# A Fourier mixing and low-rank mixer kernel: first joins of batch 0 in two pieces, one PSUM bank of the front under another tag, and a few steps of batches 1 and 2 at other places in the order

## The chip, the cores and the metric

The program runs on one core of one Trainium2 chip. The metric is the device time of one execution in microseconds (us), lower is better; several executions are summed up by their median. The engines are called as in the profile: PE (TensorE, matmuls), PEld (its weight loads), DVE (VectorE), ACT (ScalarE), POOL (GpSimd) and SP (SyncE, which here only issues DMAs).

## What is computed

`x` has the shape (8, 3136, 256) in float32, with `U` (3136, 32), `V` (32, 3136), `w_ch1` (256, 1024) and `w_ch2` (1024, 256).

```python
X = np.fft.fft(x, axis=1)
X = np.fft.fft(X, axis=2)
x = X.real.astype(np.float32)

xt = x.transpose(0, 2, 1)
h = xt @ U @ V
u = x + h.transpose(0, 2, 1)
ch = np.maximum(u @ w_ch1, 0.0) @ w_ch2
out = (u + ch).astype(np.float32)
```

## The kernel before

**Tiling.** The transform is written as matmuls with sine and cosine tables. For each of the 8 batches DVE first folds the rows of `x` (tiles `xf`, `xr`) by symmetry into `eof`, `eor`, `eos`, `ge`, `go` and `gc`; PE multiplies the folded rows by the tables into PSUM tiles named `pt`; ACT and DVE put these into two tiles `A` and `B` (bf16, 128 x 1569) and a small one, `tab`, for the low-rank product. In the odd half, `apart` makes `eh` on DVE from a copy `ev` of the first product, and `join` writes `pt + eh` and `pt - eh` into the upper parts of `A` and `B`. In the even half, `mirrored` does the same in one DVE instruction from `ev` and the second product. `chan` then transforms along the other axis (PE into `pst`, a copy to `S` or `T`), `lowrank` and `hidden` make the tiles `ta` and `qt` of the low-rank part, and `spread_rank` transposes `qt` into `qf` by a DMA transpose.

**Chunks.** The half-rows of all batches form chunks of 512 columns, counted by `c`. For each chunk `front` makes `u` = `ph` + `S` (or `T`) on DVE, one instruction for each of two halves, and starts a DMA transpose of `u` into `ut` on SP; `odd_part` makes `uo` = `S` - `T` on DVE; `direct` multiplies `u` by the first weights (PE into `p1`, ACT to `h`, line 866); `mirrors` adds `uo` and the low-rank part to the same banks (ACT to `h`, line 882); `second_product` multiplies `h` by the second weights, and DVE adds `ut` (lines 944 and 945) into `o`, which SP stores after a correction by POOL (`fx`, line 949).

**PSUM.** There are eight banks: tag `dft` has 2, `p1` has 4, `p2` has 2. A bank is given again when the last reader of its tile is done, so a matmul into a tag waits for that reader.

**Order.** Up to `order.close()` the program stands as it is written (a manual schedule): this is the front, batch 0 and the start of chunk 0. Behind it, a list of due slots (`due`, six for each chunk) says where a step of the transform of the next batch stands among the steps of the chunks: `turn(c, sl)` runs what `put` has placed at `6 * c + sl`. `transform(b)` gives the place of the first step and the list of steps; `FOLDS` gives the places of the folds. From there on PE keeps the order written; on the other engines a scheduler may move an instruction unless `tc.keep_in_program_order` pins it. `in_turn` makes `u` and `uo`, and pins them for the first chunks. `fold_tt` pins the folds.

**What the change touches.** `lrow` (line 146) lies in the pool `gen`, which `setup.close()` gives back before `cp`, the pool of `u`, `h`, `ut` and `o`, is opened; `places` (line 278) builds `EM` from `lrow` on POOL. `even_again` (line 669) makes again the first even product of batch 0, whose bank `mirrored(0, 1, cos_even)` reads. `first_u` (line 725) makes `u` of chunk 0 from columns 0 to 255 and 785 to 1040 of `A` and `B`. The DMA transposes wait for each other by semaphores, whichever queue issues them: the one of `qf` of batch 1 is issued by ACT, all the others by SP.

Of the kernel before, what the change touches and what calls it, by code (L numbers as in the profile page):

```python
# [20 lines left out]
NT = 196  # L21
# [5 lines left out]
QW = TE + NE  # L27
# [4 lines left out]
def kernel(  # L32
# [9 lines left out]
    nc = tc.nc  # L42
# [4 lines left out]
    HALF = S // 2  # L47
# [57 lines left out]
    BUFS = {"dft": 2, "p1": 4, "p2": 2}  # L105
# [37 lines left out]
    iota(jv[:], [[1, KP]], 0, 1)  # L143
    for q in (0, 2):
        load_f(x, xf, 0, q, D)
    lrow = gen.tile([P, 2, P], FP32, name="lrow")
    pcol = cpool.tile([P, 1], FP32, name="pcol")
    pint = cpool.tile([P, 1], I32, name="pint")
    iota(lrow[:], [[0, 2], [1, P]], 0)
# [128 lines left out]
    def places():  # L278

        nc.gpsimd.tensor_scalar(hm[:, 0:1], pcol[:], float(D), 0.0, op0=AL.mult, op1=AL.add)  # L280
        nc.gpsimd.tensor_scalar(hm[:, 1:2], pcol[:], -float(D), float(P), op0=AL.mult, op1=AL.add)
        for s in range(2):
            nc.gpsimd.tensor_scalar(EM[:, s * P:(s + 1) * P], lrow[:, 0, :], hm[:, s:s + 1], 1.0,
                                    op0=AL.is_equal, op1=AL.mult)
        nc.gpsimd.memset(EM[0:1, P:P + 1], 1.0)
# [164 lines left out]
    pinned = []  # L450
# [5 lines left out]

    def in_turn(c, *a, **k):
        ins = nc.vector.tensor_tensor(*a, **k)  # L458
        if pinned and c <= 2:
            tc.keep_in_program_order(ins)  # L460

    def mm(*a, **k):
# [82 lines left out]
    def seq(b, par, typ, pn, tag="dft", part=True):  # L545

        d = state(b)
        ne = NE if b else 0
        pt = psum.tile([P, QW + NE], FP32, tag=tag, name="pt", bufs=BUFS[tag])
        d["pt"] = pt  # L550
        todo = products(b, par, typ, P * typ, pn == 1, ne)
        if typ == 0 and b == 0:
            todo = todo + products(b, par, 1, 256, (pn == 1) == (par == 1), ne)
        elif typ == 0 and pn == 1:
            todo = todo + [(QW, w, rhs) for w, rhs in u_odd(b, 1, 256)]
        add_up(pt, todo)
        if pn == 0:
            ev = d["ev"] = wp.tile([P, QW], FP32, tag="ev", name="ev", bufs=EB)
            w = (2 * NT if par else TE) + ne
            nc.scalar.copy(ev[:, :w], pt[:, :w])  # L560
            if part:
                apart(b, par)

    def apart(b, par, kept=None):

        d = kept or ST[b]
        ne = NE if b else 0
        if par == 1:
            w, ev = 2 * NT + ne, d["ev"]
            eh = d["eh"] = wp.tile([P, 2 * NT], FP32, tag="eh", name="eh", bufs=2)  # L570
            nc.vector.tensor_tensor(eh[:, 0:NT], ev[:, NT - 1::-1], ev[:, w - 1:w - NT - 1:-1],
                                    op=AL.subtract)
            nc.vector.tensor_tensor(eh[:, NT:2 * NT], ev[:, 0:NT], ev[:, w - NT:w], op=AL.add)

    def join(b, par, typ, kept=None, low=True, high=True):

        d = kept or ST[b]
        ne = NE if b else 0
        pt, ev = d["pt"], d["ev"]
        dst = ST[b]["A"] if typ == 1 else ST[b]["B"]  # L580
        p_, e_ = pt[:, 0:2 * NT], d["eh"][:]
        up, dn = dst[:, 1176:784:-1], dst[:, 1177:HALF + 1]
        if low:
            nc.vector.tensor_tensor(up, p_, e_, op=AL.add)
        if not high:
            return
        if typ == 1:
            nc.vector.tensor_tensor(dn, e_, p_, op=AL.subtract)
        else:
            nc.vector.tensor_tensor(dn, p_, e_, op=AL.subtract)  # L590
        if ne:
            pu, eu = 2 * NT, NT
            nc.vector.tensor_tensor(ST[b]["tab"][:, typ, par, :].rearrange("p (g r) -> p g r", r=R),
                                    four(pt[:], pu), four(ev[:], eu), op=AL.add)
            if typ == 0:
                alt = dst[0:1, 786:HALF + 1:2]
# [33 lines left out]
    def mirrored(b, typ, kept):  # L630

        ne = NE if b else 0
        pt, ev = kept["pe"], kept["ve"]
        dst = ST[b]["A"] if typ == 1 else ST[b]["B"]
        nc.vector.scalar_tensor_tensor(strip(dst[:], 394, [[-1, 2], [2, NT]]),
                                       strip(ev[:], 1, [[NT + ne, 2], [1, NT]]), 2.0 if typ else -2.0,
                                       strip(pt[:], 1, [[NT + ne, 2], [1, NT]]),
                                       op0=AL.mult, op1=AL.subtract if typ else AL.add)
# [31 lines left out]
    def even_again(b, typ, kept):  # L670

        ev = wp.tile([P, QW], FP32, tag="ev", name="ev", bufs=EB)
        nc.scalar.copy(ev[:, :TE], kept["pe"][:, :TE])
        kept["pe"] = ev
        pt = kept["ve"] = psum.tile([P, QW], FP32, tag="p1", name="pt", bufs=BUFS["p1"])
        add_up(pt, products(b, 0, typ, P * typ, False, 0))

    def chan(b, ch, h, tag="dft", eng=None):
# [93 lines left out]

    def spread_rank(b):

        (nc.scalar if b == 1 else nc.sync).dma_start_transpose(out=QF[b % 2][:], in_=QT[:])

    def width(c):
        return min(CH, NCOL - c * CH)
# [172 lines left out]
    def transform(b):  # L951

        def odd_rows(typ, pn):
            seq(b, 1, typ, pn)
            if pn:
                join(b, 1, typ)

        def even(typ, pn):
            even_rows(b, typ, pn)
            if pn:  # L960
                mirrored(b, typ, ST[b])

        a = [lambda pn=pn: even(1, pn) for pn in range(2)]
        s = [lambda pn=pn: even(0, pn) for pn in range(2)]
        c = [lambda pn=pn: odd_rows(1, pn) for pn in range(2)]
        d = [lambda pn=pn: odd_rows(0, pn) for pn in range(2)]
        rank = [lambda: lowrank(b)]
        ch = [lambda ch=ch, h=h: chan(b, ch, h) for ch in range(2) for h in range(2)]
        q = [lambda: hidden(b)]
        if b == 1:  # L970
            return 11, [a[:1], c[:1] + a[1:], c[1:] + d[:1], s[:1] + d[1:] + s[1:],
                        [lambda ch=ch: chan(b, ch, 0, eng=nc.vector.tensor_copy) for ch in (1, 0)], ch[3:] + rank,
                        ch[1:2] + q + [lambda: spread_rank(b)]]
        if b == 2:
            return 23, [a[:1], a[1:] + c[:1], [], c[1:] + s[:1], s[1:], d[:1], d[1:], ch[:1], ch[1:2] + rank,
                        q, ch[2:3], ch[3:]]
        return 6 * (b * HALF // CH) - 15, [[x] for x in a + c + d[:1] + s + d[1:] + ch[:1] + rank + ch[1:2] + q + ch[2:]]

# [135 lines left out]
    msr = MSX[0:1].rearrange("p (l two) -> p l two", two=2)  # L1114
    nc.gpsimd.memset(msr[:, :, 0:1], -1.0)
    nc.gpsimd.memset(msr[:, :, 1:2], 1.0)
    places()
    mirror(1, slice(128, 256), AL.add)
    half(0, 1, slice(128, 256))
    seq(0, 1, 1, 0, "dft", False)  # L1120
# [3 lines left out]
    for c in range(2):  # L1124
        fourth(0, c, slice(128, 256))
    apart(0, 1, cos_odd)
    nc.gpsimd.memset(DV[:, 0:1], 0.0)
# [14 lines left out]
    load_r(x, xr, 1, 0, 2, D)  # L1142
    load_0f(1)
    mirrored(0, 0, sin_even)
    join(0, 1, 1, cos_odd, low=False)
    mirrored(0, 1, cos_even)
    nc.vector.tensor_tensor(WD[:], W1[:, 1, :], W1[:, 0, :], op=AL.subtract)
    nc.gpsimd.memset(WD[0:1], 0.0)

    due = {}  # L1150

    def put(slot, *steps):
        due.setdefault(slot, []).extend(steps)
# [113 lines left out]
```

## Time and profile before

| | |
|---|---|
| median of 3 runs | 437.91 us (436.92, 437.91, 439.9) |
| the profiled execution's own time | 436.31 us |
| its span, first to last instruction | 434.5 us |
| granted TensorE clock | 1.00 over the span |
| busy: PE, PEld | 423.8 us (98%), 284.4 us (65%) |
| busy: DVE, ACT, POOL | 319.8 us (74%), 292.2 us (67%), 125.5 us (29%) |
| DMA, mean over the span | 156 GB/s |
| chain that ended last, by engine | PE 80%, DVE 7%, DMA 7%, POOL 2% |

Times in rows are in us from the start of the span. A row of the timeline gives the start, the length, the engine, the line, the operation, out<-in, the shape and the count of equal instructions run together, and in brackets how long the engine was idle before it and what ended that. Names are cut at digits: `p` stands for `p1` and `p2`, `w` for both weights, `te`, `to` and `ts` are the tables. Matmuls overlap, and their ends are modelled, so the pace of PE is best read from one start to the next. A small q behind an engine (ACTq, SPq) marks work of its sequencer, as the issue of a DMA.

### The profile page before, as it was taken

Reading aid. Unit: us, or ns where it says so; the run is one execution under the profiler, and the core shown is the slowest. Engines: PE = TensorE matmul, PEld = TensorE weight load, DVE = VectorE, ACT = ScalarE, POOL = GpSimd, SP = SyncE. Lnnn points to the kernel's source line nnn. Section 1 sums busy time; section 2 is a strip of 40 time slices with the busy share of each in tenths; the row PEclk is TensorE's granted clock in tenths of the full one; section 3 lists DMA queues with packets and bytes.
Section 4 is the critical chain, followed back from the end, with each engine's and each line's share of the span. In section 5 each row is a group of like instructions: output and inputs, shape, how many; then the busy total and the mean of one; then the engine's idle time right before and its main releaser. Section 6 shows DMA issues by size and latency. Waiting matters only on the chain.

```text
span 434.5 us, 9406 instructions
## 1 busy us (share of the span) xinstructions
PE 423.8 (98%) x3508; PEld 284.4 (65%) x3508; DVE 319.8 (74%) x665; ACT 292.2 (67%) x633; POOL 125.5 (29%) x340
## 2 busy tenths in 40 slices
PE   5999999999999999999999999999999999999996
PEld 2774676666766766666766766666766766666675
DVE  8998989797898787769777787769777554353442
ACT  7958765666667657776667657776667657765751
POOL 8861323153234233323233142322223100011111
PEclk9999999999999999999999999999999999999999
DMA  7899798869779586727885376866334324334543
GB/s 208 210 198 217 163 273 111 203 151 244 147 163 271 102 211 177 199 74 191 175 223 155 86 181 104 217 159 146 74 88 136 100 74 113 88 122 121 122 126 121
DMA packets 89165, 67.83 MB, mean 156 GB/s; under 512 B 55402, under 2 KB 82430, under 8 KB 89118
## 3 DMA queue, kind: packets, MB, share of 16 engines
q1 hardware_dynamic: 83350, 52.79, 50.2%
q0 software_dynamic: 5472, 14.36, 13.5%
q8 instruction: 27, 0.44, 0.4%
q14 instruction: 20, 0.16, 0.1%
q10 hardware_dynamic: 296, 0.07, 0.1%
HBM read 28.86 MB, written 25.69 MB: 126 GB/s over the span
## 4 chain that ended last, share of the span: by engine, by line
PE 80%; DVE 7%; DMA 7%; POOL 2%; issue 1%; ACT 1%; SPq 0%; ACTq 0%; DVEq 0%; POOLq 0%
PE p L463 65%; PE pt L463 7%; PE pst L463 4%; DMA out_dram<-o 3%; DMA xf<-in_x_dram,xidx 2%; DVE eof L453 2%; PE ph L463 2%; DVE eor L453 2%; DMA ut<-u 1%; PE ptt L463 1%; POOL xf L57 1%; DVE u L458 1%; DVE eos L453 1%; ACT h L882 1%; PE pq L463 1%
## 5 line engine op out<-in xcount | busy, mean ns | idle before, releaser
L463 PE MATMUL p<-w,h 128*128 128x256 bf16 x1576 | 195.1, 273 | 0.0
L463 PEld LDWEIGHTS <-h 128*128 128x128 bf16 x1576 | 148.6, 98 | 39.7 <-issue 15.8
L882 ACT ACTIVATE h<-p 128x512 bf16<-128x512 f32 (+1 forms) x200 | 101.5, 595 | 83.9 <-PE p L463 77.7
L866 ACT ACTIVATE h<-p 128x512 bf16<-128x512 f32 (+1 forms) x200 | 101.8, 600 | 8.0 <-PE p L463 7.5
L463 PE MATMUL p<-u,w 128*128 128x512 bf16 (+1 forms) x400 | 93.2, 374 | 0.6 <-ACT h L882 0.4
L944 DVE TENSOR_TENSOR o<-p,ut 128x256 f32<-128x256 f32 (+1 forms) x95 | 39.6, 416 | 67.9 <-PE p L463 47.2
L949 POOL TENSOR_TENSOR o<-o,fx 128x2 f32<-128x2 f32 (+1 forms) x95 | 39.5, 416 | 155.5 <-DVE o L945 81.1
L463 PEld LDWEIGHTS <-w 128*128 128x128 bf16 x512 | 41.7, 97 | 37.8 <-issue 1.8
L463 PE MATMUL p<-uo,wd 128*128 128x512 bf16 (+1 forms) x200 | 50.8, 375 | 0.2
L458 DVE TENSOR_TENSOR u<-ph,T 128x512 bf16<-128x512 f32 (+23 forms) x63 | 34.3, 556 | 9.9 <-PE ph L463 7.9
L945 DVE TENSOR_TENSOR o<-p,ut 128x256 f32<-128x256 f32 (+1 forms) x95 | 38.9, 409 | 0.0
L453 DVE TENSOR_TENSOR eof<-xf 99x1016 bf16<-99x1016 f32 (+1 forms) x33 | 38.3, 1171 | 0.2 <-issue 0.2
L453 DVE TENSOR_TENSOR eor<-xr 99x1016 bf16<-99x1016 f32 (+1 forms) x34 | 38.4, 1143 | 0.0
L57 POOL DMA_INDIRECT xf<-in_x_dram,xidx x32 | 34.5, 1077 | 11.8 <-issue 6.7
L458 DVE TENSOR_TENSOR u<-ph,S 128x512 bf16<-128x512 f32 (+23 forms) x63 | 34.2, 554 | 0.8 <-PE ph L463 0.3
L840 POOL TENSOR_TENSOR fx<-ut 128x4 f32<-128x4 bf16 x48 | 16.0, 334 | 58.8 <-DMA ut<-u 58.8
L463 PEld LDWEIGHTS <-wd 128*128 128x128 bf16 x200 | 19.4, 98 | 13.0 <-issue 0.3
L463 PE MATMUL pt<-te,gc 98*128 98x229 bf16 (+1 forms) x196 | 24.4, 260 | 0.3 <-DVE u L458 0.3
L690 ACT CAST T<-pst 128x392 bf16<-128x392 f32 (+1 forms) x28 | 17.3, 619 | 7.3 <-PE pst L463 6.8
L463 PEld LDWEIGHTS <-gc 98*128 98x128 bf16 x220 | 19.3, 97 | 4.4 <-issue 0.7
L463 PEld LDWEIGHTS <-go 98*128 98x128 bf16 x216 | 16.5, 97 | 6.7 <-issue 0.4
L690 ACT CAST S<-pst 128x392 bf16<-128x392 f32 (+1 forms) x28 | 17.4, 623 | 3.9 <-PE pst L463 3.9
(187 smaller groups left out, 450.3 us busy)
## 6 DMA issues: line engine op xcount, KB each, us to landing
out_dram<-o SPq DMA_DIRECT2D x33, 512.0 KB
xr<-in_x_dram SPq DMA_DIRECT2D x15, 784.0 KB
out_dram<-o SPq DMA_DIRECT2D x8, 384.0 KB
out_dram<-o SPq DMA_DIRECT2D x8, 256.0 KB
out_dram<-o SPq DMA_DIRECT2D x10, 128.0 KB
xr<-in_x_dram SPq DMA_DIRECT2D x2, 392.0 KB
ut<-u SPq DMA_TRANSPOSE x48
vv<-vv SPq DMA_DIRECT2D x3, 196.0 KB
```

The source lines that it names most:

```text
L57: nc.gpsimd.indirect_dma_start(out_, None, bass.AP(t.tensor, t.offset, [[w, rows], [1, w]]), bass.IndirectOffsetOnAxis(idx, 0), element_of ...
L453: ins = nc.vector.tensor_tensor(*a, **k)
L458: ins = nc.vector.tensor_tensor(*a, **k)
L463: ins = nc.tensor.matmul(*a, **k)
L690: eng(to, pt[:, :n])
L840: nc.gpsimd.tensor_tensor(fx[:, :, 1], ut[:, 0:n, 0] if hf else ut[:, n:2 * n, 0], ut[:, n + 1:2 * n + 1, 0], op=AL.subtract)
L866: nc.scalar.activation(k["h", 0][q][:, j - 4 * q, :w], p1[:, :w], AF.Relu)
L882: nc.scalar.activation(k["h", 1][q][:, g, :w], k["p1"][g][:, :w][:, ::-1], AF.Relu)
L944: nc.vector.tensor_tensor(o[:, ts, 0:P], p2[:, :w, 0:P], ut[:rows, ts, 0:P], op=AL.add)
L945: nc.vector.tensor_tensor(o[:, ts, P:D], p2[:, :w, P:D], strip(ut[:rows], (CH // P + t0 + 1) * P, [[P, w], [-1, P]]), op=AL.add)
L949: nc.gpsimd.tensor_tensor(o[:, ts, cols], o[:, ts, cols], fx[:rows, ts, 1 - hf:], op=AL.add)
```

## The change

It has these parts:

1. `lrow` moves from the pool `gen` to `cpool`, and `places()` and the memset of `DV[:, 0:1]` on POOL move from the middle of the front to behind the last join of batch 0.
2. The lower joins of batch 0 (`up`, 392 columns) are cut at column 136: `[136:392]`, which `first_u` reads, comes first for `A` and for `B`; `[0:136]` of `B` follows at once, that of `A` after `first_u`.
3. `even_again` takes its bank from `p2` instead of `p1`.
4. Batch 1: the `eh` of the odd cosine product is made behind `mirrored` and pinned there; the DMA transpose of `qf` moves from slot 16.5 to 16.75 and is pinned on ACT.
5. Batch 2: the steps of the transform that stood at slots 23 and 24 move to 24 and 25, and the fold of `go`'s first half from 22 to 22.75 (the order of the folds stays).
6. `in_turn` pins `u` and `uo` for chunks 3 and 4 as well.

```diff
-    lrow = gen.tile([P, 2, P], FP32, name="lrow")
+    lrow = cpool.tile([P, 2, P], FP32, name="lrow")
...
     def in_turn(c, *a, **k):
         ins = nc.vector.tensor_tensor(*a, **k)
-        if pinned and c <= 2:
+        if pinned and c <= 4:
             tc.keep_in_program_order(ins)
...
-    def apart(b, par, kept=None):
+    def apart(b, par, kept=None, pin=False):
...
+            if pin:
+                tc.keep_in_program_order(ins)
...
-    def join(b, par, typ, kept=None, low=True, high=True):
+    def join(b, par, typ, kept=None, low=True, high=True, at=0, end=2 * NT):
...
-        up, dn = dst[:, 1176:784:-1], dst[:, 1177:HALF + 1]
+        up, dn = strip(dst[:], 1176, [[-1, 2 * NT]]), dst[:, 1177:HALF + 1]
         if low:
-            nc.vector.tensor_tensor(up, p_, e_, op=AL.add)
+            nc.vector.tensor_tensor(up[:, at:end], p_[:, at:end], e_[:, at:end], op=AL.add)
...
-        pt = kept["ve"] = psum.tile([P, QW], FP32, tag="p1", name="pt", bufs=BUFS["p1"])
+        pt = kept["ve"] = psum.tile([P, QW], FP32, tag="p2", name="pt", bufs=BUFS["p2"])
...
-        (nc.scalar if b == 1 else nc.sync).dma_start_transpose(out=QF[b % 2][:], in_=QT[:])
+        ins = (nc.scalar if b == 1 else nc.sync).dma_start_transpose(out=QF[b % 2][:], in_=QT[:])
+        if b == 1:
+            tc.keep_in_program_order(ins)
...
+        c0 = [lambda: seq(b, 1, 1, 0, part=False)]
...
         if b == 1:
-            return 11, [a[:1], c[:1] + a[1:], c[1:] + d[:1], s[:1] + d[1:] + s[1:],
+            return 11, [a[:1], c0 + a[1:] + [lambda: apart(b, 1, pin=True)], c[1:] + d[:1], s[:1] + d[1:] + s[1:],
                         [lambda ch=ch: chan(b, ch, 0, eng=nc.vector.tensor_copy) for ch in (1, 0)], ch[3:] + rank,
-                        ch[1:2] + q + [lambda: spread_rank(b)]]
+                        ch[1:2] + q, [lambda: spread_rank(b)]]
         if b == 2:
-            return 23, [a[:1], a[1:] + c[:1], [], c[1:] + s[:1], s[1:], d[:1], d[1:], ch[:1], ch[1:2] + rank,
+            return 23, [[], a[:1], a[1:] + c[:1], c[1:] + s[:1], s[1:], d[:1], d[1:], ch[:1], ch[1:2] + rank,
                         q, ch[2:3], ch[3:]]
...
-    places()
...
-    nc.gpsimd.memset(DV[:, 0:1], 0.0)
-    join(0, 1, 1, cos_odd, high=False)
+    join(0, 1, 1, cos_odd, high=False, at=136)
     apart(0, 1, sin_odd)
-    join(0, 1, 0, sin_odd, high=False)
+    join(0, 1, 0, sin_odd, high=False, at=136)
+    join(0, 1, 0, sin_odd, high=False, end=136)
...
     mirrored(0, 0, sin_even)
+    join(0, 1, 1, cos_odd, high=False, end=136)
     join(0, 1, 1, cos_odd, low=False)
     mirrored(0, 1, cos_even)
     nc.vector.tensor_tensor(WD[:], W1[:, 1, :], W1[:, 0, :], op=AL.subtract)
     nc.gpsimd.memset(WD[0:1], 0.0)
+    nc.gpsimd.memset(DV[:, 0:1], 0.0)
+    places()
...
-             2: (13, 13.75, 15, 15, 15, 16, 16, 16.75, 17, 19.75, 20, 20, 20, 21, 21, 22, 22.75),
+             2: (13, 13.75, 15, 15, 15, 16, 16, 16.75, 17, 19.75, 20, 20, 20, 21, 21, 22.75, 22.75),
...
-            put(16.5 if mid + n == 17 and b == 1 else mid + n, *step)
+            put({17: 16.5, 18: 16.75}.get(mid + n, mid + n) if b == 1 else mid + n, *step)
```

Line numbers move by 4 to 9: `join`'s line 584 is 588 in the changed kernel, `mirrored`'s 635 is 639, the `h` of `direct` 866 is 872, that of `mirrors` 882 is 888, the output sums 944 and 945 are 950 and 951, `qf`'s transpose 775 is 779.

The queue of ACT at the end of chunk 2, before:

```order
138 L769 COPY qt<-pq 128x256
139 L775 DMA_TRANSPOSE qf_147<-qt 128x2x128
140 L882 ACTIVATE h_1015<-p_1187 128x512
141 L882 ACTIVATE h_1015<-p_1191 128x512
142 L882 ACTIVATE h_1015<-p_1195 128x512
143 L882 ACTIVATE h_1015<-p_1199 128x512
144 L866 ACTIVATE h_1335<-p_1339 128x512
```

and in the changed kernel:

```order
138 L773 COPY qt<-pq 128x256
139 L888 ACTIVATE h_1017<-p_1189 128x512
140 L888 ACTIVATE h_1017<-p_1193 128x512
141 L888 ACTIVATE h_1017<-p_1197 128x512
142 L888 ACTIVATE h_1017<-p_1201 128x512
143 L779 DMA_TRANSPOSE qf_147<-qt 128x2x128
144 L872 ACTIVATE h_1337<-p_1341 128x512
```

The DMA transpose now stands behind the four `h` of `mirrors(2, 1)` and ahead of those of `direct(3, 0)`; its waits are the same, and SP's next transpose of `ut` still waits for it.

The queue of DVE at the transform of batch 1, before:

```order
107 L571 TENSOR_TENSOR eh<-ev 128x196
108 L573 TENSOR_TENSOR eh<-ev 128x196
109 L635 TENSOR_SCALAR A<-ev,pt 128x2x196
110 L584 TENSOR_TENSOR A<-pt,eh 128x392
111 L588 TENSOR_TENSOR A<-eh,pt 128x392
```

and in the changed kernel:

```order
109 L639 TENSOR_SCALAR A<-ev,pt 128x2x196
110 L571 TENSOR_TENSOR eh<-ev 128x196
111 L575 TENSOR_TENSOR eh<-ev 128x196
112 L588 TENSOR_TENSOR A<-pt,eh 128x392
113 L592 TENSOR_TENSOR A<-eh,pt 128x392
```

The two `eh` now follow the `mirrored` of the even product instead of preceding it.

The queue of DVE at the end of chunk 3, where the folds of batch 2 end, before:

```order
160 L453 TENSOR_TENSOR ge<-eos 99x2064
161 L944 TENSOR_TENSOR o<-p_1481,ut_1118 128x2x128
162 L453 TENSOR_TENSOR gc_115<-ge 99x4x258
163 L453 TENSOR_TENSOR gc_116<-ge 99x4x258
164 L945 TENSOR_TENSOR o<-p_1481,ut_1118 128x2x128
165 L458 TENSOR_TENSOR u_1520<-ph,S 128x512
166 L458 TENSOR_TENSOR u_1520<-ph,T 128x512
167 L453 TENSOR_TENSOR go_113<-eos 99x8x258
```

and in the changed kernel:

```order
162 L453 TENSOR_TENSOR ge<-eos 99x2064
163 L950 TENSOR_TENSOR o<-p_1483,ut_1120 128x2x128
164 L951 TENSOR_TENSOR o<-p_1483,ut_1120 128x2x128
165 L458 TENSOR_TENSOR u_1520<-ph,S 128x512
166 L458 TENSOR_TENSOR u_1520<-ph,T 128x512
167 L453 TENSOR_TENSOR gc_115<-ge 99x4x258
168 L453 TENSOR_TENSOR gc_116<-ge 99x4x258
169 L453 TENSOR_TENSOR go_113<-eos 99x8x258
```

The two halves of `u` of chunk 4 now stand ahead of the two `gc`. On PE, the four matmuls `pt<-te,gc` that stood ahead of `direct(4, 0)` stand behind it, and the eight that followed it stand one half of a `second_product` later. In chunk 3's `odd_part`, the two `uo` on DVE move from ahead of the `u` of chunk 3 to behind the second `eof` after it.

More of the change, by code (lines that the diff above doesn't have):

```diff
@@ L570, in apart @@
             eh = d["eh"] = wp.tile([P, 2 * NT], FP32, tag="eh", name="eh", bufs=2)
-            nc.vector.tensor_tensor(eh[:, 0:NT], ev[:, NT - 1::-1], ev[:, w - 1:w - NT - 1:-1],
-                                    op=AL.subtract)
-            nc.vector.tensor_tensor(eh[:, NT:2 * NT], ev[:, 0:NT], ev[:, w - NT:w], op=AL.add)
-    def join(b, par, typ, kept=None, low=True, high=True):
+            ins = nc.vector.tensor_tensor(eh[:, 0:NT], ev[:, NT - 1::-1], ev[:, w - 1:w - NT - 1:-1],
+                                          op=AL.subtract)
+            if pin:
+                tc.keep_in_program_order(ins)
+            ins = nc.vector.tensor_tensor(eh[:, NT:2 * NT], ev[:, 0:NT], ev[:, w - NT:w], op=AL.add)
+            if pin:
+                tc.keep_in_program_order(ins)
+    def join(b, par, typ, kept=None, low=True, high=True, at=0, end=2 * NT):
         d = kept or ST[b]
@@ L773, in spread_rank @@
     def spread_rank(b):
-        (nc.scalar if b == 1 else nc.sync).dma_start_transpose(out=QF[b % 2][:], in_=QT[:])
+        ins = (nc.scalar if b == 1 else nc.sync).dma_start_transpose(out=QF[b % 2][:], in_=QT[:])
+        if b == 1:
+            tc.keep_in_program_order(ins)
     def width(c):
```

## The prediction

> **What bounds the kernel now.** I read the page first, then the waits of PE, then the timeline of each stretch that the change touches. Columns of the waits: who waited on whom, us in all, times, the longest.
>
> ```profile
> span 434.5 us, 9406 instructions
> PE 423.8 (98%) x3508; PEld 284.4 (65%) x3508; DVE 319.8 (74%) x665; ACT 292.2 (67%) x633; POOL 125.5 (29%) x340
> PE pf L248 <- DVE jx L246: 5.2, 1, 5.2
> PE ptu L463 <- ACT tab L657: 0.5, 1, 0.5
> PE p L463 <- ACT h L882: 0.4, 1, 0.4
> PE pt L463 <- DVE u L458: 0.3, 1, 0.3
> PE p L463 <- ACT u L746: 0.2, 1, 0.2
> PE pt L463 <- DVE A L635: 0.2, 1, 0.2
> ```
>
> PE is busy for 423.8 of 434.5 us and sets the end. The change neither adds nor removes a matmul, so all that it can win is time in which PE waits. The wait of 5.2 us on `jx` lies at the very start and isn't touched. The other five together are 0.5 + 0.4 + 0.3 + 0.2 + 0.2 = 1.6 us: about the most that this change can save. It can lose more than that, since any wait that it adds at PE is added to the time.
>
> **The front (parts 1 to 3).** These rows, and those of all fences below that begin with a time, are timeline rows.
>
> ```profile
> 29.34 1.74 POOL L283 TENSOR_SCALAR em<-lrow,hm 128x128 bf16<-128x128 f32 x2
> 30.81 0.40 PE L463 MATMUL psu<-vv,ta 32*128 32x256 bf16 x4
> 31.29 0.73 ACT L746 CAST u<-psu 128x512 bf16<-128x512 f32 x1 [0.27 <-POOL dv L1127]
> 32.07 2.08 PE L463 MATMUL p<-u,w 128*128 128x512 bf16 x8 [0.18 <-ACT u L746]
> 36.54 0.98 DVE L1181 TENSOR_TENSOR dv<-vv 128x1567 bf16<-128x1567 bf16 x1
> ```
>
> `places` holds POOL from 29.34 to past 31.1 with the two `em`; the cast to `u` on ACT that follows is shown as released by POOL's memset of `dv`, which stands behind them, after 0.27 idle. With both moved, the cast waits only for the matmuls `psu<-vv`, which start at 30.81 and run 0.40, to 31.21. The cast started at 31.29, so 0 to 0.1 us goes here. The Trainium skill ("Perfetto Trace Analysis", "Tensor Engine Instruction (MATMUL, LD_WEIGHTS)") says that a matmul's end in a profile is an estimate; the row's 31.21 can't settle by itself which of the two came last. The two-piece joins and the bank for `even_again` can't take more than the rest of PE's stall at this place, the 0.18 ahead of `p<-u,w`, and small bank waits that the waits view doesn't list. I put the front at 0 to 0.5 us where it happens, and likeliest 0.1 to 0.3. What is left of it at the end is decided in batch 1.
>
> **Batch 1's `eh`, and what the front is worth there.**
>
> ```profile
> 63.01 0.36 DVE L571 TENSOR_TENSOR eh<-ev 128x196 f32<-128x196 f32 x1 [1.19 <-ACT ev L560]
> 63.28 0.35 ACT L622 CAST tab<-pt 128x128 bf16<-128x128 f32 x1
> 63.66 0.59 DVE L635 SCALAR_TENSOR_TENSOR A<-ev,pt 128x392 bf16<-128x392 f32 x1
> 67.81 0.68 DVE L458 TENSOR_TENSOR u<-ph,T 128x512 bf16<-128x512 f32 x1
> 68.83 0.96 PE L463 MATMUL pt<-te,gc 98*128 98x229 bf16 x8
> 70.90 0.42 DVE L944 TENSOR_TENSOR o<-p,ut 128x256 f32<-128x256 f32 x1 [0.70 <-DMA out_dram<-o]
> 73.38 0.34 PE L463 MATMUL pst<-A,mc 128*128 128x392 bf16 x1
> ```
>
> The two `eh` ran in time that DVE had idle (1.19 ahead of them). `A` (635) behind them started at 63.66, and ACT's `tab`, which reads the same PSUM tile, ended at 63.28 + 0.35 = 63.63. So `A` gains at most 0.03 from going first, and PE's wait of 0.2 on it stays. The two `eh` (63.01 to about 63.64) now stand on a DVE that is busy from 63.66 on: everything behind them comes about 0.63 later. `u`'s second half then ends at 68.49 + 0.63 = 69.12, while PE wants its bank for `pt<-te,gc` at 68.83: a new stall of about 0.3. But at 70.90 DVE had 0.70 idle, waiting for an earlier store of `o` to land, and PE's `pst<-A,mc` at 73.38 needs the DVE chain behind that. A delay of 0.63 fits into 0.70, and the new stall of PE into the stall that 73.38 has. I take 0 for the edit; if the store lands no cover, it costs 0.3. The same row limits the front: what PE wins before 70, it gives back at 73.38 as long as the store lands when it did, for DVE can't go on before it. So parts 1 to 3 are worth 0 at the end, with 0.5 as the upper end if the store moves along.
>
> **The transpose of `qf` (part 4).**
>
> ```profile
> 77.92 0.37 ACT L769 CAST qt<-pq 128x256 bf16<-128x256 f32 x1
> 79.48 1.30 ACTq L775 DMA_TRANSPOSE qf<-qt  x1
> 80.82 2.06 ACT L882 ACTIVATE h<-p 128x512 bf16<-128x512 f32 x4 [2.53 <-issue]
> 82.75 2.10 ACT L866 ACTIVATE h<-p 128x512 bf16<-128x512 f32 x4
> 79.16 1.92 PE L463 MATMUL p<-w,h 128*128 128x256 bf16 x16
> 81.47 2.06 PE L463 MATMUL p<-u,w 128*128 128x512 bf16 x8 [0.39 <-ACT h L882]
> 85.78 1.03 PE L463 MATMUL p<-uo,wd 128*128 128x512 bf16 x4
> 87.31 1.92 PE L463 MATMUL p<-w,h 128*128 128x256 bf16 x16
> 89.07 0.33 PE L463 MATMUL pst<-A,mc 128*128 128x392 bf16 x1
> 89.40 1.89 PE L463 MATMUL p<-u,w 128*128 128x512 bf16 x8
> ```
>
> ACT stood idle for 2.53 ahead of its `h` (882): from the end of `qt` at 78.29 it waited until 79.48 for the DMA order and spent 1.30 on the issue. The matmuls of these `h` are done when PE goes on at 79.16, so with the transpose behind them the four `h` start near 79.1 instead of 80.82, and end near 81.1. PE then doesn't wait: sixteen `p<-w,h` take 89.07 − 87.31 = 1.76 from start to start where nothing holds them, so `p<-u,w` starts at 79.16 + 1.76 = 80.92 instead of 81.47: 0.55. Its own eight matmuls ran 2.06 against 1.89 at 89.40, held by the later `h`: 0.17 more. Together **0.72**.
>
> Who waits for the transpose now: the issue runs on ACT from about 81.1 to 82.4, and the four `h` of `direct(3, 0)` follow it, a quarter of 2.10 each, to 82.4 + 2.1 = 84.5. PE's next writers of their four banks, `p<-uo,wd`, begin at 85.78 − 0.72 = 85.06, when all four `h` are done; the first needs only the first `h` (82.9), so 2.1 us are to spare there. SP's next transpose of `ut` waits for the landing of `qf`, a little later than before; I take nothing for it, since a chunk's `ut` is added only after its second product, many us behind. The two `uo` of this chunk, moved behind a fold of 1.2 us, would be ready well ahead of 85.06.
>
> **Batch 2 (parts 5 and 6).**
>
> ```profile
> 94.64 1.29 DVE L453 TENSOR_TENSOR gc<-ge 99x1032 bf16<-99x1032 bf16 x2
> 96.78 0.67 DVE L458 TENSOR_TENSOR u<-ph,T 128x512 bf16<-128x512 f32 x1
> 94.72 1.92 PE L463 MATMUL p<-w,h 128*128 128x256 bf16 x16
> 96.91 0.56 PE L463 MATMUL pt<-te,gc 98*128 98x229 bf16 x4 [0.27 <-DVE u L458]
> ```
>
> PE's sixteen `p<-w,h` at 94.72 free it at 94.72 + 1.76 = 96.48, but the next step, `pt<-te,gc`, started at 96.91, for its bank was read by the `u` on DVE that stood behind the two `gc`. With `u` ahead of `gc` it is ready about 1.29 earlier, and PE goes straight into `direct(4, 0)`: **0.43** gained. The two `gc` then end where the `u` ended, 97.45, and PE asks for them only after eight `p<-u,w` (1.9 us), near 98.2 on the old clock: free. Against it stands that the copies `ev` of this transform now come behind four `h` on ACT (2.07 each set), which may hold PE's next `pt` bank by about 0.1. The range of the term is 0.2 to 0.43; I take 0.33.
>
> Elsewhere (`fx` ahead of `o` on POOL, memsets) instructions move by a place or two on engines that the waits view doesn't name: 0.
>
> **Sum:** 0.72 + 0.33 + 0 + 0 = 1.05 us less. On the profiled execution's own time (436.31, span 434.5 and 1.8 around it) that is 435.3. The runs shown have 437.91 as median, and the four times with the profiled one (436.31, 436.92, 437.91, 439.9) have their middle at 437.4; I put the forecast there: 437.4 − 1.05 = **436.4**.
>
> **The rivals.** *First, slower:* the issue of the transpose holds ACT, as one of SP's did.
>
> ```profile
> 59.64 8.29 SPq L836 DMA_TRANSPOSE ut<-u  x1
> L836 SPq DMA_TRANSPOSE ut<-u x48: 1232/1301/8291, 44.9 to 421.7; - x48
> 82.76 1.04 POOL L949 TENSOR_TENSOR o<-o,fx 128x2 f32<-128x2 f32 x1 [2.76 <-issue]
> 79.78 0.19 POOL L949 TENSOR_TENSOR o<-o,fx 128x4 f32<-128x4 f32 x1
> ```
>
> The second row gives minimum, median and maximum in ns of 48 issues: the median is 1301, one took 8291. Before, the transpose sat on ACT with PE's wait at 0.4. Now the `h` of `direct(3, 0)` stand right behind it. Issued at 81.1, it decides once it takes over about 3.4 us (1.3 + 2.1); at 8.29 the first `h` ends at 81.1 + 8.29 + 0.53 = 89.9 and PE loses 89.9 − 85.06 = 4.9, net 3.8 slower: 437.4 − 1.05 + 4.9 = 441.2. At an issue of 4.5 the two cancel. For it: the issue is moved to another moment, with stores and loads about. Against it: 47 of 48 near 1.3, and so was ACT's own. Chance 0.08. [...]
>
> *Second, POOL's `em` meet DVE.* They now run about 35.5 to 37.3, beside DVE's `dv` (36.54, 0.98). The last two rows of the fence above show POOL's sum taking 1.04 in one place and 0.19 in another, with less data in the first. If such a clash holds DVE rather than POOL, `dv` and what follows lose up to one `em` (1.74 / 2 = 0.87): the time is then 437.4 − 1.05 + 0.87 = 437.2, no gain that shows. Chance 0.14. The Trainium skill ("SBUF — State Buffer", "SBUF: two separate sides") says that DVE and GpSimd share a port pair by an exclusive lock, kept for a whole instruction. By it the one that comes first keeps the other waiting, and moving `places` beside DVE's busy stretch is the wrong way.
>
> *Third, more is kept:* the store that ends DVE's idle at 70.90 moves along with the front, whose 0.5 then stays: 435.9. Chance 0.15.
>
> *Fourth, nothing is kept:* PE, freed earlier at 81.5 and 96.5, meets its next limit (DVE's folds, a landing) and gives the 1.05 back: 437.4. Against it: no wait of PE is listed behind `pt <- DVE u` at 96.91. Chance 0.13.
>
> **How the numbers follow.** The forecast has 0.5; the likeliest gives 436.4. Its terms run from 0.55 + 0.2 − 0.3 = 0.45 to 0.72 + 0.43 + 0.5 = 1.65 less. From the lowest of the four times that is 436.31 − 1.65 = 434.7; from the highest 439.9 − 1.05 = 438.9. This holds the second, third and fourth rivals too and leaves out the first and the spread of chips. One per cent is 4.4 us, about what a measurement of this kernel can tell from no change, given times from 436.31 to 439.9. Faster by more than that would need three times all of PE's waits: 0.04, for another level of the runs alone. Slower by more: the first rival, and a little for a stall that I overlooked, 0.09. The rest, 0.87, is within it.
>
> **What would show it.** Right: no `p <- ACT h` and no `pt <- DVE u` among PE's waits; ACT's `h` (882) of chunk 2 starting near 79.1, less what the front shifted; the transpose's issue near 1.3; PE's `pst<-A,mc` of batch 1 still near 73.4. Wrong: a wait of PE on `h` (872) behind the transpose, a longer `dv` or `em` near 36.5, or a stall of PE at the first `pt<-te,gc` behind batch 1's `eh` that later rows don't take back. The span should be near 433.4.

## The result and the profile after

| | before | changed |
|---|---|---|
| median of 22 runs each | 437.04 us | 435.48 us |
| lowest and highest | 435.43 to 439.9 | 434.6 to 437.51 |
| mean | 437.31 | 435.58 |
| profiled execution's own time (span) | 436.31 (434.5) | 435.61 (433.8) |

The ratio is 0.9958, with a 95% interval of 0.9943 to 0.9973: 1.2 to 2.5 us less (the two medians by themselves differ by 1.56). These are the page's head and PE's waits in the changed kernel (who waited on whom, us in all, times, the longest):

```profile
span 433.8 us, 9407 instructions
PE 423.4 (98%) x3508; PEld 284.5 (66%) x3508; DVE 319.9 (74%) x667; ACT 292.4 (67%) x633; POOL 124.3 (29%) x340
PE pf L248 <- DVE jx L246: 5.2, 1, 5.2
PE p L463 <- DVE uo L458: 0.4, 1, 0.4
PE pst L463 <- ACT S L727: 0.2, 1, 0.2
PE pt L463 <- DVE A L639: 0.2, 1, 0.2
PE ptu L463 <- ACT tab L661: 0.2, 1, 0.2
```

The waits on `h` (0.4), on `u` behind `gc` (0.3) and on the first `u` (0.2) are gone, and two that the prediction didn't have are there: `p <- DVE uo`, and `pst <- ACT S` in the front. The timeline of the changed kernel where the transpose of `qf` was:

```profile
78.63 1.09 ACT L888 ACTIVATE h<-p 128x512 bf16<-128x512 f32 x2 [0.74 <-PE p L463]
79.43 1.35 ACTq L779 DMA_TRANSPOSE qf<-qt  x1
79.60 1.09 ACT L888 ACTIVATE h<-p 128x512 bf16<-128x512 f32 x2
81.15 2.06 ACT L872 ACTIVATE h<-p 128x512 bf16<-128x512 f32 x4 [0.45 <-PE p L463]
80.52 1.89 PE L463 MATMUL p<-u,w 128*128 128x512 bf16 x8
```

The four `h` follow PE at once, and PE's eight `p<-u,w` run 1.89 with no wait. In batch 2:

```profile
89.70 2.02 POOL L57 DMA_INDIRECT xf<-in_x_dram,xidx  x1 [0.53 <-issue]
92.02 0.97 POOL L57 DMA_INDIRECT xf<-in_x_dram,xidx  x1 [0.30 <-issue]
93.01 0.37 POOL L955 TENSOR_TENSOR o<-o,fx 128x2 f32<-128x2 f32 x1
93.41 0.40 SPq L916 DMA_DIRECT2D out_dram<-o  x1
99.62 0.42 DVE L950 TENSOR_TENSOR o<-p,ut 128x256 f32<-128x256 f32 x1 [2.08 <-PE pt L463]
100.37 0.42 DVE L458 TENSOR_TENSOR uo<-S,T 128x512 bf16<-128x512 bf16 x1
100.84 1.02 PE L463 MATMUL p<-uo,wd 128*128 128x512 bf16 x4 [0.41 <-DVE uo L458]
```

The same place before:

```profile
90.32 0.99 POOL L57 DMA_INDIRECT xf<-in_x_dram,xidx  x1 [0.18 <-DVE eor L453]
93.15 0.41 SPq L910 DMA_DIRECT2D out_dram<-o  x1
99.55 0.41 DVE L458 TENSOR_TENSOR uo<-S,T 128x512 bf16<-128x512 bf16 x1
101.57 1.03 PE L463 MATMUL p<-uo,wd 128*128 128x512 bf16 x4
```

Read the first of the two from below. PE waits for `uo` of chunk 4. `uo` stands on DVE behind an `o` that began at 99.62, after 2.08 of idle time. That `o` writes into the buffer from which the store issued at 93.41 reads; in the trace this store's last part lands at 99.50. The releaser shown, a `pt` of PE, is the last wait that the profile could put a name to; in the later profiles below it is the store by name. The store was issued late, 8.75 behind the start of `mirrors(3, 0)` instead of 7.37, for POOL's correction of `o` stood behind two gathers (`DMA_INDIRECT`), and the first of these took 2.02 instead of 0.99. It took 2.00 to 2.03 in four of the 13 profiles below, those in which DVE's `eor` had begun 0.04 to 0.07 ahead of it, and 0.99 in the nine in which `eor` began 0.31 to 0.34 behind it; that the one causes the other was not tested. The stall cost PE 0.57 (start to start, against the pace of undisturbed matmuls).

The most useful reading was one of stages: the times from one of PE's marks to the next, from the starts of its rows. F is the first `ptu<-te,gc` behind 25 us to the first `p<-u,w` of `direct(0, 0)`; G from `mirrors(0, 0)` to `mirrors(0, 1)`; H from the same `ptu` to `mirrors(2, 1)`; Q from `mirrors(2, 1)` to `mirrors(3, 0)`; R from `mirrors(3, 0)` to `mirrors(4, 0)`; T from there to the end of the span. A mark is the first `p<-uo` of a `mirrors`; in seven of the profiles (before_2 to before_4, after_again, e5 to e7) that record is missing at `mirrors(2, 1)`, and the mark is put 0.215, one matmul, ahead of the next. "Start" is what lies ahead of F, from PE's first matmul on; no part of the change is in it. The kernels below the first two are the experiments of the next section.

| profiled execution | start | F | G | H | Q | R | T |
|---|---|---|---|---|---|---|---|
| before | 20.28 | 6.56 | 4.65 | 52.15 | 8.12 | 15.79 | 332.96 |
| changed | 20.08 | 6.24 | 4.74 | 51.96 | 7.40 | 16.18 | 332.96 |
| before_2 | 20.20 | 7.07 | 4.65 | 52.53 | 8.47 | 15.79 | 333.39 |
| before_3 | 20.29 | 7.06 | 4.65 | 52.39 | 8.30 | 15.79 | 333.15 |
| before_4 | 20.45 | 6.56 | 4.65 | 51.71 | 8.14 | 15.79 | 333.15 |
| after_again | 20.01 | 6.43 | 4.76 | 51.96 | 7.40 | 15.68 | 333.43 |
| e1_qf (before, `qf` moved) | 21.68 | 7.06 | 4.65 | 52.13 | 7.40 | 15.79 | 333.28 |
| e2_b2 (before, batch 2 changed) | 20.17 | 7.05 | 4.66 | 52.26 | 8.46 | 15.50 | 332.96 |
| e3_front (before, front changed) | 21.01 | 6.45 | 4.74 | 52.33 | 8.37 | 15.79 | 333.34 |
| e4_noeh (changed, `eh` back) | 20.82 | 6.39 | 4.75 | 51.92 | 7.40 | 15.61 | 333.17 |
| e5_uo (changed, `uo` earlier) | 20.07 | 6.46 | 4.75 | 52.05 | 7.40 | 15.50 | 333.03 |
| e6_nofront (changed, old front) | 20.66 | 6.65 | 4.65 | 52.02 | 7.40 | 15.50 | 333.14 |
| e7_uo_noeh (both) | 21.27 | 6.46 | 4.76 | 51.94 | 7.40 | 15.50 | 333.54 |

The start alone differs by 1.7 us from one execution to the next, more than the whole change is worth. So the spans of two profiles can't be set against each other here; their stages can.

### The profile page after: what moved, and what is told of

It is laid out like the page before. It is cut to its first block, busy times and chain, and to the rows that moved or that the text cites. A ratio compares the mean times of both kernels' runs of the same rounds, so it can differ in the third digit from the quotient of the medians.

```text
span 433.8 us, 9407 instructions
## 1 busy us (share of the span) xinstructions
PE 423.4 (98%) x3508; PEld 284.5 (66%) x3508; DVE 319.9 (74%) x667; ACT 292.4 (67%) x633; POOL 124.3 (29%) x340
## 4 chain that ended last, share of the span: by engine, by line
PE 93%; DVE 3%; ACT 2%; issue 0%; DVEq 0%; ACTq 0%
PE p L463 72%; PE pt L463 8%; PE pst L463 5%; PE fill L1049 3%; PE ph L463 2%; PE ptt L463 1%; ACT h L872 1%; PE pu L322 1%; PE pq L463 1%; PE ptu L463 0%; ACT h L888 0%; PE pf L248 0%; DVE u L458 0%; DVE pho L206 0%; PE psu L463 0%
## 5 line engine op out<-in xcount | busy, mean ns | idle before, releaser
L57 POOL DMA_INDIRECT xf<-in_x_dram,xidx x32 | 35.4, 1105 | 12.1 <-issue 7.4
L846 POOL TENSOR_TENSOR fx<-ut 128x4 f32<-128x4 bf16 x48 | 14.6, 304 | 63.0 <-DMA ut<-u 63.0
L845 POOL TENSOR_TENSOR fx<-ut 128x4 f32<-128x4 bf16 x24 | 7.3, 304 | 48.9 <-DMA ut<-u 48.9
L463 PEld LDWEIGHTS <-go 98*128 98x128 bf16 x216 | 16.5, 97 | 6.7 <-issue 0.4
```

The lines of the kernel that those rows point to most:

```text
L57: nc.gpsimd.indirect_dma_start(out_, None, bass.AP(t.tensor, t.offset, [[w, rows], [1, w]]), bass.IndirectOffsetOnAxis(idx, 0), element_of ...
L463: ins = nc.tensor.matmul(*a, **k)
L846: nc.gpsimd.tensor_tensor(fx[:, :, 1], ut[:, 0:n, 0] if hf else ut[:, n:2 * n, 0], ut[:, n + 1:2 * n + 1, 0], op=AL.subtract)
```

## The experiments

Each was timed in 12 runs beside 35 of the kernel before, the three repeats of before in one each. Differences of times below are from medians of the same session. In the expectations "`mirrors(2, 0)`", as the start of the stretch of 7.40 and of 8.1 to 8.5 us and as the end of the stretch of the front, stands for `mirrors(2, 1)`, by whose start those figures were taken.

**e1_qf: the transpose alone.**

```diff
-        (nc.scalar if b == 1 else nc.sync).dma_start_transpose(...)
+        ins = (nc.scalar if b == 1 else nc.sync).dma_start_transpose(...)
+        if b == 1:
+            tc.keep_in_program_order(ins)
...
-                        ch[1:2] + q + [lambda: spread_rank(b)]]
+                        ch[1:2] + q, [lambda: spread_rank(b)]]
...
-            put(16.5 if mid + n == 17 and b == 1 else mid + n, *step)
+            put({17: 16.5, 18: 16.75}.get(mid + n, mid + n) if b == 1 else mid + n, *step)
```

> Before with the move of the transpose of qf alone. My theory (a lead of PE is kept until a landing or the DVE chain takes it back): PE's stall ahead of the eight p<-u,w near 81.5 (0.55) and the three small ones behind it (0.17 together) go, PE is 0.72 ahead behind them, the transpose's issue takes about 1.3 us; DVE follows PE there (its u at 87.41 waited for PE's ph), so the stall of 0.44 at 96.91 stays as it is and 0.6 to 0.72 is left at the end of the span: time 0.7 lower. Rival (the lead is lost behind it, at the store that ends DVE's wait near 98.8): PE is 0.72 ahead at 90 and less than 0.3 ahead at 103. Rival (the issue holds ACT): PE waits for h (868) near 85.

Measured: 436.71 against 437.06, by the means 436.79 against 437.40, ratio 0.9983 (0.9963 to 1.0002); 0.7 less was expected. Q fell to 7.40, R stayed at 15.79: the lead of PE is kept, the issue held nobody (1.28 us here). The time's interval holds the 0.7 and no change alike, but the stage is plain: the first rival, a lead lost behind it, is out.

**e2_b2: batch 2 alone** (the two lists, `FOLDS` and `in_turn` of parts 5 and 6).

```diff
-        if pinned and c <= 2:
+        if pinned and c <= 4:
...
-            return 23, [a[:1], a[1:] + c[:1], [], c[1:] + s[:1], ...
+            return 23, [[], a[:1], a[1:] + c[:1], c[1:] + s[:1], ...
...
-             2: (..., 21, 21, 22, 22.75),
+             2: (..., 21, 21, 22.75, 22.75),
```

> Before with parts 5 and 6 (batch 2) alone. The prediction: 0.33 gained. My theory now, from the trace of the changed kernel: the stall of 0.44 at 96.9 goes, one of 0.15 for a bank that ACT's ev holds comes; the o of chunk 3 on DVE waits until the store of chunk 2's second half has landed (98.7 before), and uo of chunk 4 stands behind it, so uo is ready near 100 and PE, which wants it at 101.57 - 0.29 = 101.28, doesn't wait: 0.29 gained at 103. It waits only if the store lands after 100. Rival: uo is held by the gc and go ahead of it on DVE, not by the store: a wait of PE on uo of 0.4 or more here too, and no gain at 103 or a loss.

Measured: 436.96 against 437.06, ratio 0.9989 (0.9972 to 1.0006). R is 15.50, 0.29 below before, with no wait on `uo`: what was expected. The time can't tell so small a gain from none. The same `gc` and `go` stand ahead of `uo` here, and it began at 100.33, while PE came to it at 101.62; so the folds are not what holds it.

**e3_front: the front alone** (parts 1 to 3, as in the diff).

> Before with parts 1 to 3 (front) alone. My theory: PE is 0.3 to 0.7 ahead at 43, loses 0.2 to 0.3 of it near 59 at pt<-te,gc (DVE's fold there waits for POOL's copy, which comes when loads land, not when PE is done), and what is left at 60 stays up to 70 and is 0.3 or less at 74. Span 0 to 0.4 shorter, time 0 to 0.4 lower. The prediction had 0 at the end. Rival (the measured 1.6 comes from the front, from landings that vary less): time over 0.8 lower.

Measured: 437.14 against 437.06 by the medians, 436.98 against 437.40 by the means, and a ratio of 0.9979 (0.9961 to 0.9997). That interval, 0.1 to 1.7 us less, holds the theory's 0 to 0.4 and the rival's 0.8 alike; the stages tell more. F is 6.45. What the front does at its place shows beside e1_qf of the same session, which has the old front and an F of 7.06; first e1_qf, then e3_front:

```profile
29.43 1.62 POOL L57 DMA_INDIRECT xf<-in_x_dram,xidx  x1 [0.30 <-issue]
31.47 0.57 DVE L584 TENSOR_TENSOR B<-pt,eh 128x392 bf16<-128x392 f32 x1
31.62 0.85 PE L463 MATMUL psu<-B,msn 128*128 128x256 bf16 x4
32.41 0.40 PE L463 MATMUL psu<-vv,ta 32*128 32x256 bf16 x4
33.19 0.73 ACT L746 CAST u<-psu 128x512 bf16<-128x512 f32 x1 [0.88 <-POOL em L283]
```

```profile
28.76 1.62 POOL L57 DMA_INDIRECT xf<-in_x_dram,xidx  x1 [0.30 <-issue]
30.66 0.63 DVE L588 TENSOR_TENSOR B<-pt,eh 128x256 bf16<-128x256 f32 x2
30.95 0.60 PE L463 MATMUL psu<-B,msn 128*128 128x256 bf16 x4
31.48 0.40 PE L463 MATMUL psu<-vv,ta 32*128 32x256 bf16 x4
31.91 0.73 ACT L750 CAST u<-psu 128x512 bf16<-128x512 f32 x1 [0.28 <-PE psu L463]
```

From `psu<-B` to `psu<-vv` PE takes 0.79 with the whole join of `B` and 0.53 with the join in pieces: the last two of its four matmuls read what this join writes, and in e1_qf the third starts 0.05 behind the join's end. From `psu<-vv` to the cast it takes 0.78 with `em` ahead and 0.43 without. The two differences, 0.26 and 0.35, make the 0.61 of F. But the lead is gone at `mirrors(2, 1)` (H 52.33). The timeline of e3_front shows where:

```profile
71.80 0.42 DVE L948 TENSOR_TENSOR o<-p,ut 128x256 f32<-128x256 f32 x1 [0.96 <-DMA out_dram<-o]
74.28 0.34 PE L463 MATMUL pst<-A,mc 128*128 128x392 bf16 x1 [0.41 <-DVE tab L602]
```

DVE waits 0.96 for the store, and PE 0.41 for the chain behind it, as the prediction had it. The loss near 59 that I expected didn't come: from `p<-w,h` to `pt<-te,gc` it is 1.76 there, as before.

**e4_noeh: the changed kernel with `eh` of batch 1 ahead again.**

```diff
-            return 11, [a[:1], c0 + a[1:] + [lambda: apart(b, 1, pin=True)], c[1:] + d[:1], ...
+            return 11, [a[:1], c[:1] + a[1:], c[1:] + d[:1], ...
```

> The changed kernel with the two eh of batch 1 back ahead of mirrored; all the rest as changed. The prediction: nothing either way. My theory: the stall of PE at 68.8 (0.27, bank read by u on DVE) goes, PE comes 0.2 to 0.3 earlier to 70, and waits again at 73.1 to 73.4 for the DVE chain behind the o that waits for the store (landed 70.37): what PE has at 74 is the same within 0.1, and the time the same within 0.2. Rival (the order of eh decides how far DVE's chain gets): the stalls of 0.31 and 0.16 at 73.4 and 73.9 come back and PE is 0.3 to 0.4 later behind them than in the changed kernel.

Measured: 435.84 against 437.06, ratio 0.9972 (0.9949 to 0.9995). The timeline of it, and then of the changed kernel at the same place:

```profile
69.23 0.96 PE L463 MATMUL pt<-te,gc 98*128 98x229 bf16 x8
71.74 1.89 PE L463 MATMUL p<-u,w 128*128 128x512 bf16 x8
73.69 0.34 PE L463 MATMUL pst<-A,mc 128*128 128x392 bf16 x1
74.19 0.33 PE L463 MATMUL pst<-A,mc 128*128 128x393 bf16 x1
```

```profile
68.83 0.96 PE L463 MATMUL pt<-te,gc 98*128 98x229 bf16 x8
71.34 1.89 PE L463 MATMUL p<-u,w 128*128 128x512 bf16 x8
73.06 0.33 PE L463 MATMUL pst<-A,mc 128*128 128x392 bf16 x1
73.47 0.33 PE L463 MATMUL pst<-A,mc 128*128 128x393 bf16 x1
```

From `p<-u,w` to the second `pst<-A` it takes 2.45 with `eh` ahead and 2.13 with `eh` behind; ahead of `pt<-te,gc` the changed kernel lost 0.27 that the other didn't. Net 0.05 for the changed order: the stall moves from one side of the store's landing to the other, as my theory had it.

**The second session.** It held the changed kernel again and three variants.

> The changed kernel once more, to see which of its steps come again. My theory: the first matmul ptu<-te,gc of the front starts anywhere from 25.3 to 27 us (loads, nothing that the change touches); from there to the first p<-u,w of direct(0, 0) 6.2 to 6.5 us (before: 6.6 to 7.1); from mirrors(2, 0) to mirrors(3, 0) 7.40 (before: 8.1 to 8.5); from mirrors(3, 1) to mirrors(4, 0) 8.08 if uo was ready and up to 8.65 if the o ahead of it on DVE waited for the store, which lands 5.3 to 6.1 us after its issue. Rival (the stall on uo is no matter of the store but of DVE's folds): 8.65 again, with o started earlier than 0.2 behind the store's landing.

Measured: 435.69 against 437.25, ratio 0.9957 (0.9937 to 0.9978). R is 15.68: `uo` was in time, by little.

```profile
99.07 0.42 DVE L950 TENSOR_TENSOR o<-p,ut 128x256 f32<-128x256 f32 x1 [1.51 <-DMA out_dram<-o]
99.81 0.42 DVE L458 TENSOR_TENSOR uo<-S,T 128x512 bf16<-128x512 bf16 x1
```

The store was issued at 93.41 as in the first profile but landed at 98.94 instead of 99.50, and `o` began 0.13 behind it here and 0.12 there. So with the store issued this late the stall comes and goes with its landing. A long landing alone doesn't make it: in e2_b2 the store was issued 7.37 behind `mirrors(3, 0)` and landed 5.98 later, and `uo` was in time. Of the 0.18 and 0.11 by which R is above 15.50 here and in e4_noeh, nearly all lies at `p<-dv,qf` (near 85.6 here), the first user of the moved transpose's result, where it comes just after PE: these matmuls went on at 85.75, when SP's next transpose of `ut`, which waits for the same landing, was issued (85.76).

**e5_uo: `uo` of chunk 4 right behind `u` of chunk 4.**

```diff
             front(c + 1, 0)
+        if c == 3:
+            odd_part(4)
         turn(c, 4.75)
...
-        if c > 1:
+        if c > 1 and c != 4:
             odd_part(c)
```

> The changed kernel with uo of chunk 4 made right behind u of chunk 4, ahead of the gc, go and the o that waits for the store. My theory: no wait of PE on uo; mirrors(3, 1) to mirrors(4, 0) 8.08 us in every case, up to 0.57 less than in the profile of the changed kernel; the o still starts 0.12 behind the store's landing, and PE's next step that needs its bank has slack. Time 0 to 0.5 below the changed kernel's. Rival (DVE's folds are the bound): uo ahead makes gc 0.41 later, PE waits for pt<-te,gc instead, and the time is the same or up to 0.4 higher.

Measured: 435.32, ratio 0.9954 (0.9931 to 0.9978) against before; the changed kernel beside it had 435.69. The difference of 0.4 is within what 12 runs can't tell. The mechanism shows:

```profile
95.08 0.42 DVE L458 TENSOR_TENSOR uo<-S,T 128x512 bf16<-128x512 bf16 x1
99.06 0.42 DVE L950 TENSOR_TENSOR o<-p,ut 128x256 f32<-128x256 f32 x1 [1.20 <-DMA out_dram<-o]
100.24 1.03 PE L463 MATMUL p<-uo,wd 128*128 128x512 bf16 x4
```

`o` waits for the store as ever, but `uo` has been ready since 95.5, and `gc` 0.3 later cost PE nothing. Of all versions run this has the lowest median.

**e6_nofront: the changed kernel with the old front** (parts 1 to 3 taken back).

> The changed kernel without parts 1 to 3: the front as before, batches 1 and 2 as changed. My theory: from the first ptu<-te,gc to the first p<-u,w 6.6 to 7.1 us, with ACT's cast to u held by POOL's em by 0.3 to 0.9; 0.1 less from mirrors(0, 0) to mirrors(0, 1) than in the changed kernel; the time 0.2 to 0.5 above the changed kernel's, because the stretch up to mirrors(2, 0) gives a part of the front's 0.3 to 0.6 back. The prediction would have it at 0. Rival (the front is the larger part of the measured gain): over 0.8 above it.

Measured: 436.01, 0.32 above the changed kernel beside it; ratio to before 0.9967 (0.9946 to 0.9988). F was 6.65, at the short end of what the old front takes, and H 52.02 against 51.96. The 0.32 is what my theory had, but 12 runs can't tell it from none.

**e7_uo_noeh: e5_uo and e4_noeh together.**

> The changed kernel with uo of chunk 4 as in the run before and the two eh of batch 1 back ahead of mirrored. My theory: the time of the run with uo alone within 0.2; at pt<-te,gc behind the first half of batch 1 (near 69) no stall, at pst<-A,mc (near 73.5) stalls of 0.3 to 0.5 together. Rival (the eh at their new place win): 0.3 or more above it.

Measured: 435.97, ratio 0.9959 (0.9938 to 0.9979). It is 0.65 above e5_uo by the median and 0.3 by the mean (435.92 and 435.60); its profile had H 51.94 against 52.05, with no stall near 69 and 0.33 at `pst<-A`, as expected. That profile's span is longer than e5_uo's (434.9 and 433.3) by its start (1.2) and T (0.5), in which the two kernels have the same steps. The medians meet the rival's 0.3, the stages don't; I count the place of `eh` as undecided.

**Three more profiles of before.**

> The kernel before, profiled again: the one profile that the prediction was made from took 436.31 us, below the median of the kernel's runs. My theory: its steps were short ones by chance. From the first ptu<-te,gc to the first p<-u,w of direct(0, 0) 6.6 to 7.1 us (6.56 then); from mirrors(2, 0) to mirrors(3, 0) 8.1 to 8.5 us (8.12 then), as ACT's h behind the transpose of qf start where ut of chunk 2 has landed; from mirrors(3, 0) to mirrors(4, 0) 15.79 as then. Rival: 6.56 and 8.12 again, so that the median's further 0.7 us comes from the start, before the first ptu<-te,gc.

> As the run before, once more: 6.6 to 7.1 us, 8.1 to 8.5 us and 15.79 us by my theory; 6.56 and 8.12 by the rival.

> As the two runs before, once more: 6.6 to 7.1 us, 8.1 to 8.5 us and 15.79 us by my theory; 6.56 and 8.12 by the rival.

Times of single runs: 437.37, 436.9, 436.26. They ran on another chip than the experiments; long and short steps occur on both (F 7.06 in e1_qf, 6.65 in e6_nofront). Two of three have long steps (F 7.07 and 7.06, Q 8.47 and 8.30), the third is like the first profile (6.56, 8.14): so the theory held in two of three, and the first profile was of a shorter kind that comes again. Where the long steps come from, in before_2:

```profile
30.23 1.45 POOL L283 TENSOR_SCALAR em<-lrow,hm 128x128 bf16<-128x128 f32 x2
31.71 0.73 ACT L746 CAST u<-psu 128x512 bf16<-128x512 f32 x1 [0.90 <-POOL em L283]
79.99 0.20 POOL L839 TENSOR_TENSOR fx<-ut 128x4 f32<-128x4 bf16 x1 [4.02 <-DMA ut<-u]
80.01 1.40 ACTq L775 DMA_TRANSPOSE qf<-qt  x1
82.11 2.06 PE L463 MATMUL p<-u,w 128*128 128x512 bf16 x8 [0.74 <-ACT h L882]
```

POOL's `em` began 0.9 later than in the first profile (29.34), and ACT stood idle for 0.90 ahead of its first `u` instead of 0.27. The gather ahead of `em` had taken 1.62 instead of 1.07. It takes 1.61 or 1.62 in the seven profiles in which DVE's next `eh` begins 0.16 or 0.17 behind its start, and 1.07 or 1.08 in the six in which this `eh` begins 0.29 to 0.46 behind it; that the one causes the other was not tested. And `ut` landed at 79.9 instead of 79.4, so the transpose of `qf`, which waits for it, went 0.53 later, and PE's wait on `h` was 0.74 instead of 0.39.

## Why the prediction was right, point by point

435.48 lies within the range of 434.7 to 438.9, near its lower end; the forecast of 436.4 was 0.9 too high, and 1.05 us of gain were forecast where 1.56 were measured (interval 1.2 to 2.5). Of the 0.9, 0.4 is the base, 437.4 for 437.04, and 0.5 the gain. That the range held says little, since 437.04, no change, lies in it too; and that the gain came out no further from its forecast is in part luck, for terms that were too small met losses that weren't foreseen. The signs of being right that it named are there: no wait of PE on that `h` or on `u` behind `gc`, the four `h` from 78.63, the issue at 1.35, `pst<-A,mc` at 73.06. Of the signs of being wrong only a small one is: `dv` took 1.06 instead of 0.98. The stages tell more:

- **What bounds it.** Right: PE is at 98% in both, and every stage that moved did so through waits of PE. That the five waits, 1.6 us in all, bound the gain was too strict: they were those of one execution, and others of the same kernel have longer ones (0.7 on `h`, 0.5 on `u` in before_2).
- **Front, 0.1 to 0.3 at its place, 0 at the end.** At its place it is worth more: F is 6.86 on average over the seven executions with the old front and 6.41 over the six with the new one, 0.45, of which G takes 0.1 back. Two terms were mis-sized. The hold by POOL was put at 0 to 0.1, from an execution in which POOL came almost in time: from `psu<-vv` to the cast it was 0.48 there, but 0.77 to 0.79 in four of the seven with the old front, against 0.43 or 0.44 with the new one. And the joins in two pieces were to take no more than the 0.18 ahead of `p<-u,w` and small bank waits, but shorten the way from `psu<-B` to `psu<-vv` from 0.75 to 0.53 on average; it was 0.55 in the execution read, and the list of PE's waits doesn't show this stall. What `even_again`'s bank does by itself isn't shown. At the end little is left, as the prediction said: H is 52.17 against 52.03 on average, and the 0.14 is less than either front's own spread (51.71 to 52.53 and 51.92 to 52.33). The changed front also loses 0.26 near 59 us (`pt<-te,gc` behind `u`) in one of its six profiles, the one in which DVE had waited 0.57 for the landing of `xr` at 44.75.
- **`eh` of batch 1: 0, with a stall of 0.3 at 68.83 that 73.38 gives back.** Right in both halves: 0.27 at 68.83, and 0.32 back. Over all profiles the four with `eh` behind lose 0.26 or 0.27 there, the nine with `eh` ahead nothing, and from `p<-u,w` to the second `pst<-A` it takes 2.15 on average in the four and 2.37 in the nine (2.06 to 2.80, as the store lands).
- **Transpose of `qf`: 0.72.** The mechanism is right and the size too small: Q is 8.31 on average over the six executions with the transpose in its old place and 7.40 in all seven with it moved, 0.91. The transpose waits for the landing of `ut`, and the profile read had an early one. That it would be issued only behind the four `h`, near 81.1, was wrong (below). That nobody waits for its landing was nearly right: `p<-dv,qf` lost up to 0.17.
- **Batch 2: 0.33, between 0.2 and 0.43.** 0.29 in the four executions with nothing else in the way (15.50 against 15.79). But the step "`uo` of this chunk, ready well ahead" was checked for chunk 3 and not for chunk 4, whose `uo` stands behind an `o` that waits for a store. In the changed kernel's first profile the stall of 0.57 turned this gain into a loss of 0.39, with the 0.11 at `qf`.
- **The sum.** 0.14 + 0.91 + 0.29 = 1.34, less what the stalls at `uo` and `qf` take in some executions (0.18 and 0.68 in the two profiles of the changed kernel). That is 0.7 to 1.2, where the medians have 1.56; the differences of means of the two sessions are 1.73 and 1.55. Where the rest comes from stays open. In these profiles neither the later stages nor the start account for it: T is 333.21 on average over the six profiles with the old batch 2 and 333.18 over the seven with the new one, and the start 20.53 with the old front and 20.54 with the new. What differs in T lies in one place, where in some executions of either kernel a `p<-dv,qf` near 283 us comes up to 0.58 later, behind its transpose.
- **The rivals.** *First:* no; the issue took 1.27 to 1.53 in the seven profiles with it moved, and held nobody. *Second:* in small. `em` now runs beside `uo` and `dv` in the front; the rows of the changed kernel:

```profile
35.07 1.44 POOL L283 TENSOR_SCALAR em<-lrow,hm 128x128 bf16<-128x128 f32 x2
35.17 0.54 DVE L458 TENSOR_TENSOR uo<-S,T 128x512 bf16<-128x512 bf16 x1
35.93 1.06 DVE L1190 TENSOR_TENSOR dv<-vv 128x1567 bf16<-128x1567 bf16 x1
```

  `uo` takes 0.54 instead of 0.42 and `dv` 1.06 instead of 0.98, and PE, whose `p<-dv,qf` waits for `dv`, loses the 0.1 of G; the price of a whole `em`, 0.87, was not paid. By the Trainium skill ("SBUF — State Buffer", "SBUF: two separate sides") one of the two would have been kept out for the other's whole instruction, half of 1.44; here neither was, so the trace does not show that rule at this pair of instructions. Other pairs of this case look as if it held: in the changed kernel POOL's `fx` at 48.60 took 1.14 and ended 0.06 behind DVE's `eof`, beside which it had begun, where one at 88.97 took 0.20. *Third:* at most partly, 0.14 of the 0.5. *Fourth:* partly; part of batch 2's gain went in this way, at a landing.

## What to carry to other kernels

A stall read from one profiled execution is a sample: where the releaser is a DMA's landing or an engine that was itself held by one, profile the kernel a few times and take the stage's mean, since 0.72 became 0.91 and 0.27 of idle became 0.9. Compare stages between marks of the bound engine rather than spans. And before a producer is moved on a queue, look at what the instruction ahead of it waits for: `uo` needed nothing that was late, and still came late behind an `o` that waited for a store.

## What the hardware showed beside that

ACT issued the transpose of `qf` at 79.43, while two of the four `h` that stand ahead of it in its order had yet to run (79.60, 1.09): the issue of 1.35 us lay beside ACT's own work and cost it nothing, in e1_qf too (issue at 80.66, three `h` from 80.91). Before, with the `h` behind it, ACT stood idle for 2.53, from its wait and the issue together. So a DMA issue behind an engine's instructions can be free where one ahead of them is not.
